# A fused attention and expert kernel: C times v over 128 tokens at a time, blocks of TensorE's instructions spaced by the plan, and landmark sums as trees of additions on VectorE

## The chip, the cores and the metric

The kernel runs on one core of one Trainium2 chip. The metric is the device time of the core in microseconds (us), so less is better. Most fast runs of one kernel agree within a per cent; a run that is over 1.5% above the fastest of the same kernel counts as slow. A *ratio* in this document is the mean time of one kernel's fast runs over the mean time of the other's fast runs of the same rounds on the same chip, so it isn't quite the ratio of the medians that stand beside it.

## The reference

A landmark attention (8 batches, 8 heads, 576 tokens, 64 features, 32 landmarks) feeds a mixture of 8 experts with one expert per token. Cut to what matters here:

```python
q_lm = q.reshape(B, H, 32, 18, D).mean(axis=3)      # landmark sums: 18 tokens each
k_lm = k.reshape(B, H, 32, 18, D).mean(axis=3)
A  = softmax(q @ k_lm.T);  Bm = softmax(q_lm @ k_lm.T);  C = softmax(q_lm @ k.T)
Z  = Bm.T / (norm1(Bm) * norminf(Bm))
for _ in range(6):
    Z = 2 * Z - Z @ Bm @ Z                           # the "W" chain, 6 steps
x = A @ Z @ C @ v                                    # C @ v: 32 x 576 times 576 x 64 per head
# then for each token: relu(x @ w1[e]) @ w2[e], scaled by a gate; e = argmax(x @ w_gate)
```

With the inputs used here all tokens of a batch go to one expert, and batches 2, 3 and 5 have the same expert as the batch two before, so their weight loads are skipped at run time (20 of 32 weight transfers are executed).

## The kernel before

The kernel isn't a loop written by hand. It lists its operations for all 8 batches with engine, estimated duration, what they read and write, and buffers; a small list scheduler in Python (the *plan*) then picks the order in which they are emitted, engine by engine. The instructions are unrolled, so TensorE executes one straight stream of about 9,400 records. A change of any number in the plan can reorder everything.

The scheduler's core takes, of the operations that can start first, the one with the best priority:

```python
for o in lst:
    s = max(f, o.ready)
    ...
    cands.append((s, o, picks))
...
order.sort(key=lambda o: o.start)
```

Landmark sums: one of two engines makes them, whichever the plan finds free. VectorE reduces the 18 tokens of each landmark with one strided instruction; GpSimd makes a tree of five additions through a scratch tile:

```python
def total(e, t=t, sums=sums, x=x):
    src = t.ap[:, 2 * x:2 * x + 2]
    if e == "DVE":
        nc.vector.tensor_reduce(sums.ap, src.rearrange("p j (x t) -> p j t x", x=g), axis=AX, op=ALU.add)
        return
    add = nc.gpsimd.tensor_tensor
    add(tr, src[:, :, 0:288], src[:, :, 288:576], op=ALU.add)
    for n in (128, 64, 32):
        add(tr[:, :, 0:n], tr[:, :, 0:n], tr[:, :, n:2 * n], op=ALU.add)
    add(sums.ap, tr[:, :, 0:32], tr[:, :, 256:288], op=ALU.add)
op(("DVE", "POOL"), {"DVE": 1.35, "POOL": 3.4}, "sum", total, ...)
```

C times v: nine chunks of 64 tokens. Two heads lie in the two halves of the partitions, so each matmul has 64 rows by 32 columns of the array:

```python
def flip(dst, c):                                    # transposes of C, 64 tokens of two heads at once
    nc.tensor.transpose(dst, in_=Cexp.ap[:, c].rearrange("p i t -> p (i t)"), identity=ident)
def valC(x):
    for c in (range(5) if x == 0 else range(5, 9)):
        src = Ct.ap if c == 4 else CT.ap[:, c // 5, 128 * (c % 5):128 * (c % 5) + 128]
        for j in range(J):                           # J = 4
            for i in range(I):                       # I = 2
                nc.tensor.matmul(pV.ap[quad(j), i, 0:D], lhsT=src[half(i), quad(j)], rhs=vt.ap[half(i), c, j, :],
                                 start=(c == 0), stop=(c == 8))
```

In the trace each of these fp32 matmuls stands as two weight loads and two matmuls: 72 matmuls a batch are 144 matmul records and 144 weight loads (1,152 of each in 8 batches), 288 instructions.

The softmax here doesn't subtract the row's maximum and nothing guards it: scores larger than these inputs give would overflow.

Of the kernel before, what the change touches and what calls it, by code (L numbers as in the profile page):

```python
# [22 lines left out]
F32 = mybir.dt.float32  # L23
# [5 lines left out]
ALU = mybir.AluOpType  # L29
# [25 lines left out]
class Op:  # L55
    __slots__ = ("eng", "dur", "lat", "fn", "deps", "succ", "new", "use", "kind", "b", "kb", "prio", "seq", "left", "start",
                 "end", "done", "ready", "tiled", "bias", "choice", "durs")


class Plan:  # L60


    LAT = {"PE": 0.27, "DVE": 0.09, "ACT": 0.12, "POOL": 0.12, "SP": 0.05}

    def __init__(self, model):
        self.ops, self.writer, self.m = [], {}, model

    def op(self, eng, dur, fn, kind, b, r=(), w=(), new=(), use=(), kb=0.0, tiled=False, bias=0.0):
        o = Op()
        deps = []  # L70
        for key in r:
            for p in self.writer[key]:
                if p not in deps:
                    deps.append(p)
        o.choice = eng if isinstance(eng, tuple) else (eng,)
        o.eng = o.choice[0]
        o.durs = {}
        for e in o.choice:
            o.durs[e] = self.m["dur"].get(kind + "@" + e, self.m["dur"].get(kind, dur[e] if isinstance(dur, dict) else dur))
        o.dur, o.lat, o.fn, o.deps, o.succ = o.durs[o.eng], self.LAT[o.eng], fn, deps, []  # L80
        o.new, o.use, o.kind, o.b, o.kb, o.seq, o.tiled, o.bias = list(new), list(use), kind, b, kb, len(self.ops), tiled, bias
        for t in o.new + o.use:
            t.users.append(o)
        for p in deps:
            p.succ.append(o)
        for key in w:
            self.writer.setdefault(key, []).append(o)
        self.ops.append(o)
        return o

    def run(self):
# [40 lines left out]
        n_left = len(ops)  # L132
        order = []
        slack = m["slack"]

# [30 lines left out]
        while n_left:  # L166
            best = None
            for e, lst in avail.items():
# [5 lines left out]
                for o in lst:  # L174
                    s = max(f, o.ready)
                    picks = ()
                    if first is not None and s > first + slack:
                        continue
                    if o.new:
                        rm = room(o)  # L180
                        if rm is None:
                            continue
                        s = max(s, rm[0])
                        picks = rm[1]
                    if o.kb and e == "SP" and len(lanes) >= m["lanes"]:
                        s = max(s, lanes[-m["lanes"]])
                    cands.append((s, o, picks))
                    if first is None or s < first:
                        first = s
# [16 lines left out]
            if o.eng == "PE" and o.tiled != pe_tiled:  # L206
                at += 0.09
                pe_tiled = o.tiled
            o.start, o.end = at, at + o.dur
            free[o.eng] = o.end  # L210
# [29 lines left out]

    def emit(self):
        for o in self.order:
            for t in o.new:
                t.make()
            o.fn() if len(o.choice) == 1 else o.fn(o.eng)


MODEL = {"period": 12.0, "stretch": 1.3, "slack": 0.1, "rate": 405.0, "lanes": 8,
         "dur": {"Mhi": 0.22, "expA": 0.66, "expB": 0.29, "expC": 0.52, "ezx": 0.28, 
                 "An": 0.76, "BT": 0.26, "P0": 0.23, "rd": 0.62, "upd": 0.29, "Mlo": 0.23,  # L250
                 "Cv0": 0.9, "Cv1": 0.72, "MT": 0.2, "Mg": 0.12, "Mw": 0.52, "W": 0.2, "colsum": 0.12, "gram": 0.16, "pG": 0.65,
                 "pb": 0.98, "pd": 0.58, "scC0": 0.68, "scC1": 0.55, "scA": 0.57},
         "off": {"H": 10, "Y": 10, "Y4": 10, "y": 10, "y4": 10, "st": 10}, "again": (2,)}
SPY = []
# [4 lines left out]
def attention_then_experts(ctx: ExitStack, tc, qt, kt, vv, gates, w, out):  # L259
# [29 lines left out]
    tag(sb, "qT", 3, [128, J, S])  # L289
    tag(sb, "v", 3, [128, 9, J, D])  # L290
    tag(sb, "ks", 6, [128, 2, m])
    tag(sb, "qs", 6, [128, 2, m])
    tag(sb, "Cexp", 1, [128, 9, I, 64])
    tag(sb, "CT", 1, [128, 2, 512])
# [57 lines left out]
    for e in range(E):  # L352
        nc.gpsimd.memset(iota8[:, e:e + 1], float(e))
    tr = cp.tile([128, 2, 288], F32)
    wg = cp.tile([128, J, 2 * E], F32)
# [37 lines left out]
    def batch(b):  # L393
# [8 lines left out]
        for x in range(2):  # L402
            for which, t, src in (("k", kT, kt), ("q", qT, qt)):
                def ld(t=t, src=src, x=x):
# [3 lines left out]
                    use=[t] if x else [])  # L408
        dma("ldv", lambda: nc.sync.dma_start(out=vt.ap.rearrange("p c j d -> p (c j d)"), in_=vv[b]), 128 * 2304 * 4, w=[("v", b)], new=[vt])
        if b == 0:  # L410
# [7 lines left out]
        for x in range(2):  # L418
            for which, t, sums in (("k", kT, ks[x]), ("q", qT, qs[x])):
                def total(e, t=t, sums=sums, x=x):  # L420
                    src = t.ap[:, 2 * x:2 * x + 2]
                    if e == "DVE":
                        nc.vector.tensor_reduce(sums.ap, src.rearrange("p j (x t) -> p j t x", x=g), axis=AX, op=ALU.add)  # L423
                        return
                    add = nc.gpsimd.tensor_tensor
                    add(tr, src[:, :, 0:288], src[:, :, 288:576], op=ALU.add)
                    for n in (128, 64, 32):
                        add(tr[:, :, 0:n], tr[:, :, 0:n], tr[:, :, n:2 * n], op=ALU.add)  # L428
                    add(sums.ap, tr[:, :, 0:32], tr[:, :, 256:288], op=ALU.add)
                op(("DVE", "POOL"), {"DVE": 1.35, "POOL": 3.4}, "sum", total, r=[(which, b, x)], w=[("s" + which, b)], new=[sums],  # L430
                   use=[t])
# [3 lines left out]

        CW = (320, 256)

        def score(lo, n, p, lm, tok, with_b):
# [4 lines left out]
            if with_b:  # L443
                for j in range(J):
                    for i in range(I):
                        nc.tensor.matmul(p.ap[quad(j), i, 320:320 + m], lhsT=qs[j // 2].ap[half(i), j % 2, :],
                                         rhs=ks[j // 2].ap[half(i), j % 2, :])
        for hf in range(2):
            op("PE", 0.65 if hf == 0 else 0.53, f"scC{hf}", lambda hf=hf: score(320 * hf, CW[hf], psC[hf], qs, kT, hf == 0),
               r=[("k", b), ("sq", b)] + ([("sk", b)] if hf == 0 else []), w=[("pC", b, hf)], new=[psC[hf]],  # L450
# [5 lines left out]
        for i in range(I):  # L456
            def expB(i=i):
                nc.scalar.activation(out=Bme.ap[:, i], in_=psC[0].ap[:, i, 320:320 + m], func=ACTF.Exp, scale=scale / (g * g),
                                     accum_out=st.ap[:, 4 + i:5 + i])
            op("ACT", 0.31, "expB", expB, r=[("pC", b, 0)], w=[("Bme", b)], new=[] if i else [Bme, st],  # L460
               use=[psC[0]] + ([Bme, st] if i else []))
        for hf in range(2):
            for i in range(I):
                def expC(hf=hf, i=i):
                    nc.scalar.activation(out=Cexp.ap[:, 5 * hf:5 * hf + CW[hf] // 64, i, :], in_=psC[hf].ap[:, i, 0:CW[hf]].rearrange(
                                             "p (c t) -> p c t", t=64), func=ACTF.Exp,
                                         scale=scale / g, accum_out=st.ap[:, 2 * hf + i:2 * hf + i + 1])
                op("ACT", 0.50, "expC", expC, r=[("pC", b, hf)] + ([("Bme", b)] if hf + i == 0 else []), w=[("Cexp", b, hf)],
# [71 lines left out]

        def flip(dst, c):
            nc.tensor.transpose(dst, in_=Cexp.ap[:, c].rearrange("p i t -> p (i t)"), identity=ident)  # L542
        for x in range(2):
            def turn(x=x):
                for c in range(4):
                    flip(pT.ap[:, x, 128 * c:128 * c + 128], 5 * x + c)
            op("PE", 0.48, "turn", turn, r=[("Cexp", b, x)], w=[("pT", b, x)], new=[] if x else [pT],
               use=[Cexp] + ([pT] if x else []))

            def cpy(e, x=x):  # L550
# [5 lines left out]
               new=[] if x else [CT], use=[pT] + ([CT] if x else []))  # L556
        op("PE", 0.15, "turn4", lambda: flip(at_[:, 0:128], 4), r=[("Cexp", b, 0)], w=[("pt", b)], new=[pt], use=[Cexp])
        op(EITHER, {"ACT": 0.27, "DVE": 0.29}, "Ct", lambda e: (nc.scalar.copy if e == "ACT" else nc.vector.tensor_copy)(
# [4 lines left out]
        def valC(x):  # L563
            for c in (range(5) if x == 0 else range(5, 9)):
                src = Ct.ap if c == 4 else CT.ap[:, c // 5, 128 * (c % 5):128 * (c % 5) + 128]
                for j in range(J):
                    for i in range(I):
                        nc.tensor.matmul(pV.ap[quad(j), i, 0:D], lhsT=src[half(i), quad(j)], rhs=vt.ap[half(i), c, j, :],  # L568
                                         start=(c == 0), stop=(c == 8))
        for x in range(2):  # L570
            op("PE", 1.1 - 0.2 * x, f"Cv{x}", lambda x=x: valC(x),
               r=[("CT", b, x), ("v", b)] + ([("pV", b, 0)] if x else [("Ct", b)]),
               w=[("pV", b, x)], new=[] if x else [pV], use=[CT, vt] + ([pV] if x else [Ct]), tiled=True)
        op("DVE", 0.3, "Cvn", lambda: nc.vector.tensor_tensor(
# [205 lines left out]
    plan.run()  # L780
    plan.emit()
    region.__exit__(None, None, None)
# [77 lines left out]
```

## Time and profile before

| | before |
|---|---|
| median, range of 4 runs | 289.74 us, 289.31 to 291.3 |
| profiled span, mean granted TensorE clock | 291.3 us, 0.895 |
| TensorE matmul busy | 231.7 us (80%) |
| TensorE records in order | 9,429 |
| stops at edges of 256 instructions (below) | 25.2 us |

The page of the profile, kernel before: the busy times with their share and instruction counts, the granted clock in 40 slices of the span (tenths), the chain of waits by engine, and three groups of instructions (busy time and mean ns of one, then the idle time of the engine before them and what ended it).

```profile
span 291.3 us, 10745 instructions
PE 231.7 (80%) x4685; PEld 135.7 (47%) x4686; DVE 168.1 (58%) x420; ACT 78.0 (27%) x240; POOL 62.7 (22%) x147
...
PEclk9999558857978999999589997999999979989997
...
PE 70%; DVE 11%; issue 11%; DMA 4%; ACT 2%; ACTq 0%
...
L568 PE MATMUL big<-v,CT 64*32 64x64 f32 x1024 | 15.4, 225 | 17.7 <-issue 17.7
...
L441 PE MATMUL big<-kT,qs 64*32 64x256 f32 (+1 forms) x256 | 16.1, 511 | 11.8 <-DVE qs L423 11.8
...
L423 DVE TENSOR_REDUCE qs<-qT 128x64 f32<-128x1152 f32 x11 | 23.4, 2123 | 0.0
```

TensorE is the busiest engine and the chain runs mostly through it. But 11% of the chain is "issue": time in which TensorE waited for nothing that the profile shows. Line 568, C times v, has most of it. Line 441, the scores, waits for the landmark sums, both times at the very start: the first eight matmuls begin at 9.1 us, the rest of the first scores at 13.1.

The waits of TensorE, kernel before (engine and line, what it waited for, us in total, times, longest):

```profile
PE big L568 <- issue: 18.6, 8, 4.5
PE big L441 <- DVE qs L423: 11.8, 2, 9.1
PE big L597 <- issue: 5.0, 2, 2.8
...
PE bank L520 <- issue: 1.6, 1, 1.6
```

One such wait in order of time, kernel before (start us, us, engine, line, tile, count, and in brackets the idle time):

```profile
25.20 0.81 PE L568 MATMUL big<-v,CT 64*32 64x64 f32 x59
30.00 0.43 PE L568 MATMUL big<-v,CT 64*32 64x64 f32 x5 [3.99 <-issue]
```

TensorE stops for 4 us in the middle of a group of like matmuls, which makes a missing operand unlikely. If all TensorE records are sorted by start and numbered from 0, all eleven issue gaps over 0.3 us come before record numbers that leave 193 when divided by 256 (worked out from the trace's records):

```
record   705  1729  2497  2753  3777  5057  6081  6337  7361  8385  8641
mod 256  193   193   193   193   193   193   193   193   193   193   193
gap us  3.99  1.59  0.36  4.46  0.86  3.28  2.06  2.76  0.97  2.62  2.25     sum 25.2
```

That is the reading: TensorE stops at the edge of a block of 256 instructions. The trace has a DMA queue of the kind "instruction" that fits it: 39 packets of 16,384 bytes, 0.9 to 2 us each, for 37 edges. Most start 0.1 to 4 us after an edge, a few only shortly before the next. And at each of the eleven stops TensorE resumes 1.3 to 1.5 us after the end of such a packet (for the first: the packet ends at 28.67 us, TensorE resumes at 30.00), while edges without a stop lie anywhere from 0.5 to 10.6 us behind the newest packet (the last edge, near the end, 20.7). How long TensorE took for a block, the stop left out, can be worked out from the same records: all six blocks that took under 3 us ended in a stop, and none that took over 5.7 us did. So, in this reading, a block executed too quickly ends before the next one is there.

### The profile page before, as it was taken

The numbers are of one execution on the slowest core, as the hardware profiler recorded it, in microseconds if no ns is written. First come the engines' busy times: TensorE is split into PE (matmuls) and PEld (weight loads), VectorE is DVE, ScalarE is ACT, GpSimd is POOL, SyncE is SP. The second block draws the span as 40 slices with busy tenths as digits, with TensorE's granted clock in tenths as the row PEclk, the third lists the DMA queues.
The fourth block names the chain that finished last, engine by engine and source line by source line (L and its number), as shares of the span: only waits on it lengthen the run. The fifth ranks groups of instructions, "written<-read, shape, count | busy, mean of one in ns | idle before, by whom it ended". The sixth has DMA issues, their size and how long they took to land.

```text
span 291.3 us, 10745 instructions
## 1 busy us (share of the span) xinstructions
PE 231.7 (80%) x4685; PEld 135.7 (47%) x4686; DVE 168.1 (58%) x420; ACT 78.0 (27%) x240; POOL 62.7 (22%) x147
## 2 busy tenths in 40 slices
PE   0385586689769998995999949998999399599890
PEld 0134444444444556544655636456645364253440
DVE  3774566785429678575286615664766154354730
ACT  1041032044201362231242504231605041220400
POOL 7386209257440008004001200000020002100000
PEclk9999558857978999999589997999999979989997
DMA  7999929957990484347402980130039602963132
GB/s 264 418 415 412 415 59 303 296 160 213 267 281 19 149 301 141 145 135 284 164 2 88 198 169 7 37 129 4 2 84 229 144 3 38 246 174 115 47 110 65
DMA packets 14601, 49.06 MB, mean 168 GB/s; under 512 B 1744, under 2 KB 2768, under 8 KB 13520
## 3 DMA queue, kind: packets, MB, share of 16 engines
q1 hardware_dynamic: 11664, 37.79, 34.7%
q0 software_dynamic: 2880, 10.49, 18.9%
q8 instruction: 39, 0.64, 0.9%
q14 instruction: 18, 0.15, 0.2%
HBM read 61.90 MB, written 9.44 MB: 245 GB/s over the span
## 4 chain that ended last, share of the span: by engine, by line
PE 70%; DVE 11%; issue 11%; DMA 4%; ACT 2%; ACTq 0%
PE mo L376 18%; PE mo L722 14%; PE big L441 7%; PE bank L520 6%; PE big L568 5%; PE big L597 4%; DVE ks L423 4%; PE mo L386 3%; PE big L542 3%; DVE qs L423 3%; PE mo L379 3%; DMA out_dram<-y 2%; PE bank L648 2%; PE bank L586 2%; DMA kT<-in_kt_dram 1%
## 5 line engine op out<-in xcount | busy, mean ns | idle before, releaser
L376 PE MATMUL mo<-wb,hT 128*128 128x512 bf16 x256 | 60.6, 383 | 0.1
L722 PE MATMUL mo<-A,P 128*128 128x288 f16 x256 | 48.7, 336 | 1.3 <-ACT P L713 0.7
L728 ACT ACTIVATE hT<-mo 128x288 bf16<-128x288 f32 x67 | 27.4, 411 | 64.4 <-PE mo L722 63.0
L376 PEld LDWEIGHTS <-hT 128*128 128x128 bf16 x256 | 23.5, 99 | 26.9 <-issue 2.3
L730 DVE TENSOR_SCALAR hT<-mo 128x288 bf16<-128x288 f32 x61 | 27.8, 457 | 14.1 <-PE mo L722 12.9
L748 DVE TENSOR_SCALAR y<-mo,cmain 128x512 f32<-128x512 f32 (+1 forms) x34 | 24.4, 717 | 18.8 <-PE mo L376 16.5
L722 PEld LDWEIGHTS <-P 128*128 128x128 bf16 x256 | 26.2, 112 | 17.5 <-issue 6.1
L568 PE MATMUL big<-v,CT 64*32 64x64 f32 x1024 | 15.4, 225 | 17.7 <-issue 17.7
L698 POOL COPY cmain<-coef 128x5 f32 x8 | 1.5, 190 | 118.9 <-DVE coef L696 94.8
L520 PE MATMUL bank<-cur 32*32 32x64 f32 (+1 forms) x768 | 21.4, 229 | 5.4 <-issue 1.6
L441 PE MATMUL big<-kT,qs 64*32 64x256 f32 (+1 forms) x256 | 16.1, 511 | 11.8 <-DVE qs L423 11.8
L524 DVE SCALAR_TENSOR_TENSOR cur<-cur,bank 128x128 f32<-128x128 f32 (+1 forms) x48 | 13.0, 271 | 20.5 <-PE bank L520 16.3
L423 DVE TENSOR_REDUCE qs<-qT 128x64 f32<-128x1152 f32 x11 | 23.4, 2123 | 0.0
L520 PEld LDWEIGHTS bank<-cur 32*32 32x32 f32 x768 | 13.4, 112 | 20.7 <-issue 4.6
L568 PEld LDWEIGHTS big<-v,CT 64*32 64x32 f32 x1024 | 11.6, 105 | 20.6 <-issue 18.9
L428 POOL TENSOR_TENSOR tr<-tr 128x256 f32<-128x256 f32 (+2 forms) x39 | 19.5, 500 | 3.1
L602 DVE TENSOR_TENSOR A<-Aexp,big 128x576 f16<-128x576 f32 x16 | 11.8, 748 | 14.0 <-PE big L597 14.0
L713 ACT CAST P<-mo 128x512 bf16<-128x512 f32 x16 | 9.4, 585 | 37.1 <-PE mo L386 37.0
L423 DVE TENSOR_REDUCE ks<-kT 128x64 f32<-128x1152 f32 x8 | 17.1, 2132 | 3.7 <-DMA kT<-in_kt_dram 3.7
L597 PE MATMUL big<-rd,bsel 32*128 32x72 f32 x256 | 13.9, 363 | 5.1 <-issue 5.0
L597 PEld LDWEIGHTS big<-rd,bsel 32*128 32x128 f32 x256 | 12.1, 262 | 7.4 <-issue 5.4
L386 PE MATMUL mo<-wb,Mt 64*32 64x512 bf16 x256 | 11.8, 410 | 3.5 <-ACT y L746 2.6
(98 smaller groups left out, 274.6 us busy)
## 6 DMA issues: line engine op xcount, KB each, us to landing
wb<-in_w_dram POOLq DMA_DIRECT2D x32, 512.0 KB
kT<-in_kt_dram SPq DMA_DIRECT2D x16, 576.0 KB, 5.7
qT<-in_qt_dram SPq DMA_DIRECT2D x16, 576.0 KB, 10.1
v<-in_vv_dram SPq DMA_DIRECT2D x8, 1152.0 KB, 8.9
out_dram<-y SPq DMA_DIRECT2D x32, 256.0 KB, 2.1
out_dram<-y SPq DMA_DIRECT2D x8, 128.0 KB, 3.9
wg<-in_gates_dram SPq DMA_DIRECT2D x1, 32.0 KB, 11.8
```

Of the source, the lines that this page charges most:

```text
L376: nc.tensor.matmul(pY, lhsT=lhsT, rhs=w2[:, fc, :], start=(fc == 0), stop=(fc == FC - 1))
L386: nc.tensor.matmul(pP[i][quad(j), :], lhsT=Mt[half(i), b, x, j, :], rhs=w1[half(i), fh, j, :], start=(x == 0), stop=(x == 1))
L423: nc.vector.tensor_reduce(sums.ap, src.rearrange("p j (x t) -> p j t x", x=g), axis=AX, op=ALU.add)
L428: add(tr[:, :, 0:n], tr[:, :, 0:n], tr[:, :, n:2 * n], op=ALU.add)
L441: nc.tensor.matmul(p.ap[quad(j), i, 0:n], lhsT=lm[j // 2].ap[half(i), j % 2, :], rhs=tok.ap[half(i), j, lo:lo + n])
L520: nc.tensor.matmul(spv(0, 2 * m)[quad(r), i, lo:], lhsT=src.ap[quad(r), i, 0:m], rhs=src.ap[quad(r), i, lo:])
L568: nc.tensor.matmul(pV.ap[quad(j), i, 0:D], lhsT=src[half(i), quad(j)], rhs=vt.ap[half(i), c, j, :], start=(c == 0), stop=(c == 8))
L597: nc.tensor.matmul(pb[i].ap[:, hf, QS * s:QS * s + QS], lhsT=bsel[qd, s].rearrange("p a b -> p (a b)"), rhs=rd.ap[qd, :])
L722: nc.tensor.matmul(pH.ap[:, 0:HS], lhsT=P.ap[:, i, fc * 128:fc * 128 + 128], rhs=A[:, b, i, HS * hf:HS * hf + HS], start=(i == 0), stop=(i ...
L728: nc.scalar.activation(out=o, in_=pH.ap[:, 0:HS], func=ACTF.Relu)
L730: nc.vector.tensor_scalar(out=o, in0=pH.ap[:, 0:HS], scalar1=0.0, scalar2=None, op0=ALU.max)
L748: nc.vector.tensor_scalar(out=y.ap[:, 0:wd], in0=pY.ap[:, 0:wd], scalar1=cmain[:, b, c:c + 1], scalar2=None, op0=ALU.mult)
```

## The change

It has three parts.

1. C times v over 128 tokens at a time. Four chunks of 128 tokens and a rest of 64 replace nine of 64, with the layouts of v, C and the transposes changed to suit (also on the host). A batch has 160 instructions for it instead of 288.
2. The plan: it counts TensorE's instructions, and delays in its model any operation that would cross an edge of 256 less than 3.6 us after the edge before, so that others go first. It makes later batches' sums less urgent (`pen`), and knows that the weight loads of batches 2, 3 and 5 are skipped, not that of 2 alone.
3. VectorE makes its landmark sums by the tree of five unit-stride additions too, with its own scratch tile.

The diff, cut to its core:

```diff
+    INS = {"scC0": 64, "scC1": 32, "scA": 32, ..., "Cv0": 64, "Cv1": 96, ...}   # instructions of an operation
+        o.ins, o.pen = self.INS.get(kind, 0) + 1, pen * self.m["pen"]
+        block, fetch = 256, m["fetch"]
+        count, crossed = 0, 0.0
+        def stall(o, at):
+            if o.eng != "PE" or count // block == (count + o.ins) // block:
+                return 0.0
+            return max(0.0, crossed + fetch - at - o.dur * (block - count % block) / o.ins)
+                    if e == "PE":
+                        s += stall(o, s)
+                    s += o.pen
-MODEL = {..., "again": (2,)}
+MODEL = {..., "fetch": 3.6, "fill": (0.0, 0.7, 0.08), "pen": 0.5, ..., "again": (2, 3, 5)}   # this fill emits nothing
...
-                    if e == "DVE":
-                        nc.vector.tensor_reduce(sums.ap, src.rearrange("p j (x t) -> p j t x", x=g), axis=AX, op=ALU.add)
-                        return
-                    add = nc.gpsimd.tensor_tensor
+                    add, tr = (nc.vector if e == "DVE" else nc.gpsimd).tensor_tensor, trs[e]
-                op(("DVE", "POOL"), {"DVE": 1.35, "POOL": 3.4}, "sum", total, ...
+                op(("DVE", "POOL"), {"DVE": 1.5, "POOL": 3.6}, "sum", total, pen=1.0 if b else 0.0, ...
...
-        CW = (320, 256)
+        CW = (256, 320)
-    nc.tensor.transpose(dst, in_=Cexp.ap[:, c].rearrange("p i t -> p (i t)"), identity=ident)
+    nc.tensor.transpose(dst, in_=Cexp.ap[:, i, lo:lo + n], identity=ident)
+        def turn4():                                  # the last 64 tokens, one matmul per head
+            for i in range(I):
+                nc.tensor.matmul(at_[half(i), 0:128], lhsT=Cexp.ap[:, i, 512:576], rhs=ident)
...
-            for c in (range(5) if x == 0 else range(5, 9)):
+            for c in (range(2) if x == 0 else range(2, 5)):
                 for j in range(J):
                     for i in range(I):
+                        if c == 4:
+                            nc.tensor.matmul(o, lhsT=Ct.ap[half(i), quad(j)], rhs=vt.ap[half(i), 2048 + D * j:...], ...)
+                        else:
+                            lo = 256 * (c % 2) + 128 * i + m * j
+                            nc.tensor.matmul(o, lhsT=CT.ap[:, x, lo:lo + m], rhs=vt.ap[:, 512 * c + 256 * i + D * j:...], ...)
```

## The prediction

> **What bounds it now.** By the busy table TensorE takes 231.7 of 291.3 us (80%), VectorE 58%. The chain of waits is 70% TensorE, 11% VectorE and 11% "issue" (about 31 us). The waits view names the issue time: 18.6 us before the C times v matmuls, 5.0 before the spread of the row sums, 1.6 before a W step. Numbering TensorE's records in order, eleven gaps (0.4 to 4.5 us, 25.2 us in all) stand at numbers that leave 193 when divided by 256: TensorE stops at the edge of a block of 256 instructions. [...] 39 packets of 16,384 bytes on an instruction queue, each about 1 us. [...] A stopped edge follows the edge before by mostly 4.8 to 6.7 us. C times v, 288 instructions a batch in about 2.2 us, empties a block faster than one is fetched.
>
> **What changes.**
> 1. C times v: 144 to 80 matmuls a batch. Before, 15.1 ns each (64 in 0.97 us). The new form (128 rows by 32 columns, 64 moving) resembles the row sums (32 in 0.64 us, 20 ns at 72): estimate 18 ns, so 2.2 to about 1.4 us; the last transpose grows by about 0.2 us. -4.5 us in all.
> 2. Instructions: about -120 of 1,180 a batch, four fewer edges in all and a shorter burst: transposes, row sums, C times v and spread go from 434 to 320.  Stops: 25 to about 7 us, so -18.
> 3. The plan's block counter starts at zero and counts one extra per operation, about 50 a batch, where the trace has about 7 semaphore records a batch and the first edge at record 193. So its edges drift from the true ones; I credit the spacing with little.
> 4. Landmark sums on VectorE: 19 reductions of 2.13 us. A five-step tree, estimated from the 0.15 to 0.75 us of other additions, is about 1.6 us. But both inputs lie in SBUF: [...] the Bme addition took 0.77 us instead of 0.22 beside GpSimd's trees, a 2-element addition 0.71 instead of 0.15. GpSimd's selects run until 9 us, its trees until 138: I expect the gain to vanish: 0, give or take 2 us. The first scores still begin near 13 us.
> 5. Fewer stops may keep the clock up (mean grant 0.895; about 50 us at half after the start): -2 us.
>
> These are on the chain, so nearly all counts: 289.9 - 18 - 4.5 - 2 + 1.5 (new waits on VectorE and ScalarE) = 267 us.
>
> **Prediction: 267 us, 256 to 281. Faster by over 2%: 0.93; within 2%: 0.06; slower: 0.01.**
>
> **To check.** C times v records 640 instead of 1,152, about 11 us of chain; issue idle on TensorE below 10 us, what is left at edges of 256; VectorE's first tree additions (128x576) near 0.7 us alone, over 1 us beside GpSimd; the last 40 us (two experts' dense matmuls) unchanged.
>
> **What would make it wrong.** The edges fall badly and stops of 3 to 4 us stay; blocked trees delay the W chain; or the new order starves the experts' matmuls of weights, or the clock is halved more often.

289.9 - 18 - 4.5 - 2 + 1.5 comes to 266.9. The 2 us of item 5 are an estimate beside two figures of the trace. What before's trace shows of it: up to the last matmul there are seven half-clock stretches, 58 us in all. Six begin during one of the eleven stops or at most 0.5 us after it, the seventh 1.7 us after a wait of 2.6 us for ScalarE; beside the other five stops (0.4 to 2.6 us) the clock records stand at 1.0.

## The result

| | before | after |
|---|---|---|
| median, range of 4 runs | 289.74 us, 289.31 to 291.3 | 275.5 us, 274.2 to 276.49 |
| ratio | | 0.950 (95%: 0.944 to 0.955) |
| profiled span, clock | 291.3 us, 0.895 | 274.3 us, 0.924 |
| TensorE records | 9,429 | 8,452 |
| stops at edges | 25.2 us | 7.7 us |

The kernel is 5% faster, inside the predicted range, 8.5 us above the predicted median. The page after (line numbers have moved: 599 is C times v, 464 the scores; 449 the tree's first addition, 451 its next three):

```profile
span 274.3 us, 9860 instructions
PE 220.1 (80%) x4197; PEld 127.2 (46%) x4198; DVE 160.9 (59%) x462; ACT 80.0 (29%) x244; POOL 86.4 (31%) x177
...
PEclk9999579759997999999979997999999759999999
...
PE 68%; DVE 17%; issue 5%; POOL 4%; ACT 3%; POOLq 0%; DVEq 0%; ACTq 0%
...
L464 PE MATMUL big<-kT,qs 64*32 64x256 f32 (+1 forms) x256 | 15.5, 528 | 14.5 <-POOL qs L452 14.5
...
L451 DVE TENSOR_TENSOR trDVE<-trDVE 128x256 f32<-128x256 f32 (+2 forms) x39 | 20.1, 515 | 1.3
```

Issue on the chain fell from 11% to 5%, but VectorE on it rose from 11% to 17%, and GpSimd came onto it with 4%. C times v no longer stands with idle time, as its group by form shows (kernel after):

```profile
L599 PE MATMUL big<-v,CT 128*32 128x64 f32 x512 | 11.0, 223 | 0.7 <-ACT CT L577 0.4 <-issue 0.3
```

The waits of TensorE, kernel after:

```profile
PE big L464 <- POOL qs L452: 14.5, 1, 14.5
PE bank L542 <- issue: 6.7, 4, 3.7
PE big L644 <- DVE A L634: 4.3, 4, 3.0
PE mo L402 <- DVE y L780: 3.6, 1, 3.6
PE big L662 <- DVE Mt L652: 2.7, 2, 2.0
```

The first scores now wait for a sum by GpSimd until 14.5 us (before: for VectorE's, until 9.1 us for the first eight matmuls and 13.1 for the rest), and there are new waits of 3 to 4 us on VectorE. The plan also moved sums: VectorE makes 13 of the 32 and GpSimd 19, where it was 19 and 13 before. The longest, for an output scaling (y), ends at 86 us. VectorE in order of time just before it, kernel after:

```profile
77.17 0.75 DVE L449 TENSOR_TENSOR trDVE<-qT 128x576 f32<-128x576 f32 x1
77.95 2.57 DVE L451 TENSOR_TENSOR trDVE<-trDVE 128x256 f32<-128x256 f32 x3
80.62 0.43 DVE L452 TENSOR_TENSOR qs<-trDVE 128x64 f32<-128x64 f32 x1
81.08 0.90 DVE L449 TENSOR_TENSOR trDVE<-kT 128x576 f32<-128x576 f32 x1
82.02 2.56 DVE L451 TENSOR_TENSOR trDVE<-trDVE 128x256 f32<-128x256 f32 x3
84.61 0.50 DVE L452 TENSOR_TENSOR ks<-trDVE 128x64 f32<-128x64 f32 x1
85.04 0.34 DVE L652 TENSOR_TENSOR Mt<-big,Mt 128x64 bf16<-128x64 f32 x2
85.30 2.05 DVE L780 TENSOR_SCALAR y<-mo,cmain 128x512 f32<-128x512 f32 x3
```

and GpSimd in the same time, kernel after:

```profile
77.32 0.78 POOL L452 TENSOR_TENSOR ks<-trPOOL 128x64 f32<-128x64 f32 x1
78.17 1.46 POOL L449 TENSOR_TENSOR trPOOL<-kT 128x576 f32<-128x576 f32 x1
79.72 1.65 POOL L451 TENSOR_TENSOR trPOOL<-trPOOL 128x256 f32<-128x256 f32 x3
81.45 0.71 POOL L452 TENSOR_TENSOR ks<-trPOOL 128x64 f32<-128x64 f32 x1
82.24 1.46 POOL L449 TENSOR_TENSOR trPOOL<-qT 128x576 f32<-128x576 f32 x1
```

Two sums took VectorE from 77.17 to 85.11 us, 7.9 us, where two reductions take 4.2 (experiment 1). The two engines take turns: GpSimd's 64-element addition takes 0.78 us instead of 0.32, as it ends only after VectorE's first (at 77.92 us); VectorE's middle three take 2.57 us, as they sit behind GpSimd's 1.46 us. All 13 trees of VectorE in this trace, put in order by how long GpSimd executed an instruction that reads SBUF (where the operands of both engines' additions lie) beside them (worked out from the records):

```
beside GpSimd us   0.00  0.00  0.00  0.00 | 1.76  1.95  1.99 | 2.51  2.72 | 3.43  3.49  3.55  3.64
the tree took us   2.05  2.05  2.05  2.12 | 2.34  2.17  2.21 | 2.90  3.11 | 3.89  3.88  3.94  4.03
```

A tree by itself takes 2.05 us, and the reduction it replaces 2.13. So it gains next to nothing alone, and costs up to 1.9 us beside GpSimd. (The 1.95 and 1.99 are short GpSimd selects at the start; there it was GpSimd that was held up, its 16 selects of line 375 took 6.7 us instead of 5.6.) Not every instruction of VectorE was held up: before's 19 reductions took 2.08 to 2.20 us with up to 2.1 us of GpSimd beside them, and the 16 instructions A<-Aexp,big of the kernel after, which take one input from a tile that TensorE writes, 0.74 to 0.76 us with and without GpSimd.

The idle time of TensorE in both traces, all worked out from the matmul records (first start, gaps between, end):

| us | before | after | change | the prediction's term |
|---|---|---|---|---|
| stops at edges | 25.2 | 7.7 | -17.5 | -18 |
| matmuls busy | 231.7 | 220.1 | -11.6 | -4.5 and -2 (clock) |
| other idle up to the last matmul | 27.4 | 40.9 | +13.5 | +1.5 |
| after the last matmul | 7.1 | 5.5 | -1.5 | |
| span | 291.3 | 274.3 | -17.0 | -23 |

Each number is rounded by itself. The table compares one profiled run of each kernel, and before's, at 292.9 us, was 3.2 us above its median: the medians differ by 14.2 us, not by 17. A stop is any gap over 0.3 us at an edge; one of after's, 1.05 us, is put down to ScalarE by the profile.

### The profile page after: what moved, and what is told of

Its sections match the earlier page's. It is cut to its first block, busy times and chain, and to the rows that moved or that the text cites. A ratio compares the mean times of both kernels' runs of the same rounds, so it can differ in the third digit from the quotient of the medians.

```text
span 274.3 us, 9860 instructions
## 1 busy us (share of the span) xinstructions
PE 220.1 (80%) x4197; PEld 127.2 (46%) x4198; DVE 160.9 (59%) x462; ACT 80.0 (29%) x244; POOL 86.4 (31%) x177
## 4 chain that ended last, share of the span: by engine, by line
PE 68%; DVE 17%; issue 5%; POOL 4%; ACT 3%; POOLq 0%; DVEq 0%; ACTq 0%
PE mo L402 20%; PE mo L754 11%; PE big L464 8%; PE bank L542 6%; DVE trDVE L451 5%; PE big L629 3%; PE mo L405 3%; PE mo L412 3%; PE big L564 3%; PE big L599 3%; DVE hT L762 2%; DVE trDVE L449 2%; POOL bsel L375 2%; PE bank L680 2%; PE bank L618 2%
## 5 line engine op out<-in xcount | busy, mean ns | idle before, releaser
L754 PE MATMUL mo<-A,P 128*128 128x288 f16 x256 | 44.7, 306 | 4.6 <-DVE hT L762 2.2
L754 PEld LDWEIGHTS <-P 128*128 128x128 bf16 x256 | 23.2, 103 | 18.8 <-issue 10.0
L451 POOL TENSOR_TENSOR trPOOL<-trPOOL 128x256 f32<-128x256 f32 (+2 forms) x57 | 29.9, 525 | 4.5
L702 POOL DMA_DIRECT2D wb<-in_w_dram x24 | 6.9, 289 | 72.1 <-DMA wb<-in_w_dram 56.6
L464 PE MATMUL big<-kT,qs 64*32 64x256 f32 (+1 forms) x256 | 15.5, 528 | 14.5 <-POOL qs L452 14.5
L546 DVE SCALAR_TENSOR_TENSOR cur<-cur,bank 128x128 f32<-128x128 f32 (+1 forms) x48 | 12.9, 269 | 18.9 <-PE bank L542 9.1
L451 DVE TENSOR_TENSOR trDVE<-trDVE 128x256 f32<-128x256 f32 (+2 forms) x39 | 20.1, 515 | 1.3
L449 POOL TENSOR_TENSOR trPOOL<-qT 128x576 f32<-128x576 f32 x13 | 18.8, 1449 | 0.7 <-issue 0.2
L481 ACT ACTIVATE Bme<-big 128x32 f32<-128x32 f32 x16 | 3.0, 193 | 44.1 <-PE big L469 44.1
L488 ACT ACTIVATE Cexp<-big 128x256 f32<-128x256 f32 (+1 forms) x32 | 12.9, 412 | 4.2 <-PE big L464 4.2
L778 ACT ACTIVATE y<-mo,cmain 128x256 f32<-128x256 f32 (+1 forms) x10 | 5.6, 560 | 27.8 <-PE mo L405 20.1
L743 DVE CAST P<-mo 128x512 bf16<-128x512 f32 x16 | 10.9, 684 | 4.4 <-PE mo L412 4.3
```

What stands on the lines that cost most here:

```text
L464: nc.tensor.matmul(p.ap[quad(j), i, 0:n], lhsT=lm[j // 2].ap[half(i), j % 2, :], rhs=tok.ap[half(i), j, lo:lo + n])
L488: nc.scalar.activation(out=Cexp.ap[:, i, 256 * hf:256 * hf + CW[hf]], in_=psC[hf].ap[:, i, 0:CW[hf]], func=ACTF.Exp, scale=scale / g, accu ...
L546: nc.vector.scalar_tensor_tensor(out=dst.ap[:, :, lo:], in0=src.ap[:, :, lo:], scalar=2.0, in1=spv(0, 2 * m)[:, :, lo:], op0=ALU.mult, op1 ...
L754: nc.tensor.matmul(pH.ap[:, 0:HS], lhsT=P.ap[:, i, fc * 128:fc * 128 + 128], rhs=A[:, b, i, HS * hf:HS * hf + HS], start=(i == 0), stop=(i ...
```

## Experiments

Theory 1: the stops are instruction fetch at edges, the short C times v removed them, and the trees on VectorE gave back about 10 us because they and GpSimd's trees exclude each other. Rivals: the stops are waits for C times v's operands; the gain is the plan's spacing; the new waits come of the new order. Three calls of four kernels, each on one chip, with the kernel before run beside them. Medians below are of fast runs. In the first call (experiments 1 to 4) 3 of 8 runs of before were slow, in the third (9 to 12) 4 of 7; there the record's verdict is "unclear" for the kernels that have a ratio, and runs 2 and 12, each with two slow runs of four, have none. In the second call (5 to 8) all four kernels are "faster".

### 1. After, with reductions on VectorE, order unchanged

```diff
+                    if e == "DVE":
+                        nc.vector.tensor_reduce(sums.ap, src.rearrange("p j (x t) -> p j t x", x=g), axis=AX, op=ALU.add)
+                        return
                     add, tr = (nc.vector if e == "DVE" else nc.gpsimd).tensor_tensor, trs[e]
```

> The kernel after, with its order of instructions unchanged, but each landmark sum that VectorE makes is the single strided reduction of before again (13 of them). Theory 1 (the trees' two SBUF inputs exclude GpSimd's trees, so VectorE is blocked and the new waits of TensorE on VectorE are paid for by that): the reductions take 2.1 us each whatever GpSimd does, GpSimd's first additions go back to 1.41 us, the first scores start near 13 us instead of 14.5, and the whole takes 268 to 273 us against 275.5. Rival (the new waits come of the new order, the trees themselves gain 0.3 to 0.6 us each): 276 to 280 us.

Measured: 265.4 us (264.5 to 268.2), ratio to before 0.917 (0.908 to 0.926), against 0.950 (0.944 to 0.955) for the kernel after in another call: the intervals don't touch. GpSimd's first additions take 1.41 us again (1.87 for the first of them in the kernel after), and the first scores begin at 12.9 us, though they wait for the same sum by GpSimd as in the kernel after:

```profile
PE big L467 <- POOL qs L455: 12.9, 1, 12.9
```

The place of the two sums on VectorE, this kernel:

```profile
74.45 2.13 DVE L449 TENSOR_REDUCE qs<-qT 128x64 f32<-128x1152 f32 x1
76.51 2.14 DVE L449 TENSOR_REDUCE ks<-kT 128x64 f32<-128x1152 f32 x1
78.58 0.34 DVE L655 TENSOR_TENSOR Mt<-big,Mt 128x64 bf16<-128x64 f32 x2
78.84 2.05 DVE L783 TENSOR_SCALAR y<-mo,cmain 128x512 f32<-128x512 f32 x3
```

Two sums take 4.2 us instead of 7.9. As the order is the same, the two streams of weight loads can be laid on each other: the trees' kernel is 1.6 us behind at the first score, 2.7 us at 76 us, 7.3 us at 88 us, 11.2 at 141 us, after GpSimd's last trees, and 11.7 at the end. So theory 1 holds, and more strongly than expected: the time is below my 268 to 273. Of the 11.4 us between the two spans, 8.1 are idle time of TensorE, and 4.9 are matmul busy time (34 us at half clock against 41); stops are 1.4 longer. Two half-clock stretches that only the trees' kernel has, 86.0 to 89.4 us and 137.2 to 140.6, begin at or just after the end of a stop in which TensorE waits for VectorE behind a tree (3.6 us until 86.09, 2.2 until 136.07). Whether the stops caused them isn't shown.

### 2. Before, with trees on VectorE, order unchanged

```diff
-                    if e == "DVE":
-                        nc.vector.tensor_reduce(...)
-                        return
-                    add = nc.gpsimd.tensor_tensor
+                    add, tr = (nc.vector if e == "DVE" else nc.gpsimd).tensor_tensor, trs[e]
```

> The kernel before, order unchanged, but each sum on VectorE is the tree of five additions (19 of them). Theory 1 (blocking): the first tree additions on VectorE take over 0.9 us where a GpSimd tree runs; the first scores start no earlier than 12 us; 289 to 294 us in all. Rival (the tree is a gain of about 0.5 us for each of the sums, most of which are on the chain): 282 to 286 us.

Measured: 291.5 us (fast: 290.7 and 292.4; two slow runs at 296), before 291.1. No gain for 19 trees, as theory 1 said, and the rival's 282 to 286 is out. First scores begin at 9.4 and 13.7 us, 0.3 and 0.6 later than before; I had said no earlier than 12. Thirteen of the 19 trees had at most 2.1 us of GpSimd beside them and took 2.05 to 2.32 us; the worst, beside 3.67 us of GpSimd, took 4.05. Against reductions of 2.13 us the 19 trees took VectorE 8.3 us more in all, nearly the 9.0 us of the 13 trees in the kernel after. In this trace TensorE's other idle time is 33.4 us, 6 more than before's, but matmuls are busy 3.6 us less and stops 1.9 us shorter. So the trees weren't free here either; the rest made up for them, and one trace of each can't say whether by chance. That the same part costs nothing in the total of one order and 10 us in another is worth remembering.

### 3. Before, with the edges moved by half a block

```diff
+        for _ in range(64):
+            filler()          # nc.tensor.matmul(bank[0:32, 384:385], lhsT=onesb[:, 0:32], rhs=onesb[:, 0:1])
         for o in self.order:
```

> The kernel before with 64 tiny matmuls (128 records) ahead of everything, in the time when TensorE waits for the first data. They move the edges of the blocks of 256 by half a block against the program. Theory (stops stand at the edges of instruction blocks): all issue gaps over 0.3 us still stand at record numbers that leave 193 when divided by 256, which is now at other instructions; their sum changes, 15 to 32 us; the time 283 to 297 us. Rival (they are waits for an operand of C times v): the gaps stay at the same matmuls of the program, now 65 over a multiple of 256, and the time stays within 1 us of 289.7.

Measured: 288.6 us, ratio 0.991 (0.980 to 1.002). All twelve issue gaps stand at numbers that leave 193 or 194 (this trace lacks a few matmul records, so it is numbered by its weight loads), 24.9 us in all, but now they come before other instructions. The waits of TensorE, this kernel:

```profile
PE big L570 <- issue: 12.0, 4, 4.1
PE big L443 <- DVE qs L425: 9.1, 2, 6.4
PE bank L522 <- issue: 6.1, 3, 3.3
PE bank L588 <- issue: 5.6, 3, 2.8
```

Line 588 is the row sums, which hadn't one issue gap before, and 522 the W chain. The program's instructions and operands are the same; only their numbers differ. So the stops belong to the numbers and not to C times v: what C times v does is to make the blocks short in time. The operand rival falls. The time decides nothing here; the places of the gaps do.

### 4. After, without the spacing

```diff
-"fetch": 3.6
+"fetch": 0.0
```

> The kernel after with the plan's spacing of blocks turned off (its fetch time set to 0), all else as it is. Theory (the plan's edges drift from the true ones, the win is from fewer instructions): stops at edges sum to 5 to 14 us and the time is 272 to 281 us. Rival (the spacing is what removed the stops): stops of 18 us or more and 284 to 290 us.

Measured: 280.6 us, ratio 0.966 (0.959 to 0.972); stops 7.8 us, with spacing 7.7. The spacing isn't what removed the stops. The kernel is still 5 us slower than the one after (in another call), at the same stops. Its order is another one: in the traces 3.1 us of the difference are matmul busy time (51 us at half clock against 41) and 2.3 us other idle time. So the spacing was worth something here, but not by its stops.

### 5. Before, with C times v over 128 tokens alone

The layouts, transposes, widths and matmuls of the change; sums, costs and plan settings as before.

In words:

```diff
 (of the kernel after)
-"fetch": 3.6 ... "pen": 0.5 ... "again": (2, 3, 5)
+"fetch": 0.0 ... "pen": 0.0 ... "again": (2,)
 and the reduction of experiment 1, with {"DVE": 1.35, "POOL": 3.4}
```

> The kernel before with one part of the change alone: C times v over 128 tokens (its layouts, transposes and score widths), with the landmark sums, the costs and the plan settings of before. Theory (shorter instruction bursts are the gain, the trees a loss): stops at edges fall from 25 to 10 us or less, C times v records from 1,152 to 640, 264 to 275 us, so at least as good as the whole change. Rival (the parts need each other, the plan's spacing above all): stops over 15 us, 278 us or more.

Measured: 264.9 us, ratio 0.905 (0.901 to 0.910); the profiled run was a slow one (268.3). Stops 8.8 us. The waits of TensorE, this kernel:

```profile
PE big L467 <- DVE qs L449: 12.0, 2, 9.1
PE bank L545 <- DVE rd L624: 4.1, 6, 2.3
PE big L632 <- issue: 3.8, 3, 2.3
PE big L598 <- issue: 3.3, 1, 3.3
```

Blocks that took TensorE under 3 us: two, both with a stop, where before had six. From before's trace to this one stops fall by 16.4 us and matmul busy time by 10.7, other idle time grows by 3.7. One part alone gives more than the whole change.

### 6. Before, with the plan part alone

```diff
+spacing (3.6 us; "turn4": 2, "Cv0": 160, "Cv1": 128), "pen": 0.5, "again": (2, 3, 5)
```

> The kernel before with the plan part alone: spacing of blocks at 3.6 us with counts for the old C times v, delay of later batches' sums, and the three skipped weight loads known. Theory (its edges drift from the true ones and 288 instructions of C times v can't be spaced): stops at edges 18 us or more, 283 to 292 us. Rival (spacing works by itself): stops under 12 us, 280 us or less.

Measured: 277.3 us, ratio 0.947 (0.941 to 0.953); stops 15.3 us (a slow run's trace). A miss: I expected 283 to 292 and stops of 18 or more. The time is the rival's (280 or less), the stops (under 12) are nobody's. On the old kernel the plan part does work.

### 7 and 8. The plan told the truth, without and with edges where the trace has them

Both are the kernel of experiment 1 with the first batch's sums held on VectorE and a reduction costed at 2.05 us; the second has besides:

```diff
-o.ins = self.INS.get(kind, 0) + 1;    count, crossed = 0, 0.0;   "fetch": 3.6
+o.ins = self.INS.get(kind, 0) + 0.13; count, crossed = 67, 0.0;  "fetch": 5.4
```

> The kernel after with VectorE's sums as single reductions, the plan told what such a one takes (2.05 us), and the first batch's four sums held on VectorE, because in the kernel after one of them went to GpSimd, which is busy with constants until 9 us. Theory: the first scores begin by 13.3 us; about even with the same kernel without this (265.4 us), 261 to 268 us; stops at edges 4 to 14 us, as the order is new. Rival (the order of after is what made 265 possible): over 270 us.

> As the run before, and the plan's edges put where the trace has them: the counter starts at 67 instead of 0, counts 0.13 instead of 1 extra per operation, and an edge costs 5.4 us instead of 3.6. Theory (the spacing did little because its edges were in the wrong places): stops at edges under 4 us in all and 2 to 8 us less than the run before. Rival (the order can't be spaced: too little else is ready in the bursts): stops within 3 us of the run before, and no gain.

Measured: 266.4 us (ratio 0.909, 0.906 to 0.913) without, 268.8 us (0.917, 0.912 to 0.921) with. Stops 9.1 us in both. With the sums held on VectorE the first eight matmuls of the scores begin at 8.9 us and the rest at 12.9, where experiment 1 has all at 12.9; the whole gained nothing by it. The expectation of stops under 4 us is a miss, and the rival holds: with edges in the right places the plan still can't space them. One stop shows why. In every kernel with the new C times v the longest stop is one of 3.2 to 3.7 us at the last batch's C times v; the kernel after:

```profile
212.97 0.68 PE L599 MATMUL big<-v,CT 128*32 128x64 f32 x32
213.59 0.34 PE L595 MATMUL big<-v,Ct 64*32 64x64 f32 x16
217.67 0.43 PE L542 MATMUL bank<-cur 32*32 32x32 f32 x16 [3.73 <-issue]
```

It stays with and without spacing, and with either count of edges (3.4 and 3.6 us). That too little other work was ready there is my reading; no run shows it.

### 9 and 10. Spacing alone, and the known skips alone, on the kernel before

```diff
+"fetch": 3.6                                  (run 9, "pen": 0.0, "again": (2,))
-"again": (2,)
+"again": (2, 3, 5)                            (run 10)
```

> The kernel before with the plan's spacing of blocks alone (3.6 us, counts for the old C times v), neither the delay of the sums nor the three known skips. The whole plan part gave 14.7 us, against my theory. Theory 2 (spacing works although its edges drift, because it breaks up the bursts anywhere): most of that gain is here, stops at edges 12 to 18 us, 276 to 283 us. Rival (the gain is of the other two settings): stops over 22 us, 286 us or more.

> The kernel before with one setting changed: the plan knows that the weight loads of batches 2, 3 and 5 are skipped, not of 2 alone. Theory 2 (the gain of the plan part is the spacing): within 3 us of before, stops at edges 20 to 30 us. Rival (knowing the skips lets the experts' matmuls come earlier and fill the bursts): 279 to 285 us, stops under 20 us.

Measured: spacing alone 283.2 us, ratio 0.978 (0.961 to 0.996), stops 19.4 us, where I said 276 to 283 and 12 to 18: both just missed. Known skips alone 280.8 us, ratio 0.979 (0.958 to 1.000), before 290.6; stops 22.3 us. That's a miss: I had said within 3 us of before. The rival's time (279 to 285) fits, its stops (under 20) don't. Both settings help the old kernel about equally, and the first reduces stops by about 6 us. The second's gain is mainly in matmul busy time, 221.3 us against 231.7, with the clock at half for 34 us instead of 58 us (clock records of the trace, from the first matmul to the last; the stretch before the first record, at 21 to 22 us, isn't counted). Why the order keeps the clock up was not tried.

### 11 and 12. With the new C times v: without and with the plan part, on one chip

Both have reductions on VectorE, costed at 2.05 us; the second has spacing, `pen` and the three skips.

```diff
-{"DVE": 1.35, "POOL": 3.4}      (run 11: of experiment 5)     -{"DVE": 1.5, "POOL": 3.6}   (run 12: of experiment 1)
+{"DVE": 2.05, "POOL": 3.4}                                    +{"DVE": 2.05, "POOL": 3.4}
```

> C times v over 128 tokens alone (the plan settings of before, reductions on VectorE), the plan told that a reduction takes 2.05 us instead of 1.35. Theory (C times v is the whole gain): 262 to 270 us. It is the partner of the next run on the same chip.

> As the run before plus the whole plan part (spacing, delay of sums, three known skips). Theory (with the short C times v the plan part adds nothing clear: the bursts are already short, stops stay at 7 to 11 us in both): within 3 us of the run before. Rival (the parts add up, the plan part was worth 14.7 us on the kernel before): 5 us or more below it, stops under 4 us.

Measured: 265.8 us without (four runs from 265.2 to 266.3; ratio to before 0.919, 0.907 to 0.931). With the plan part the two fast runs are 267.0 and 270.1, and two slow ones 271.8 and 273.2: no gain, perhaps a small loss. Stops 9.3 and 6.5 us. The parts don't add up: what the plan part was worth on the old kernel isn't there to be had once C times v is short.

### All together

| kernel | fast median us | ratio to before | stops us |
|---|---|---|---|
| after (all three parts) | 275.5 | 0.950 | 7.7 |
| trees alone (2) | 291.5 | fast medians as before's | 23.3 |
| plan alone (6) | 277.3 | 0.947 | 15.3 |
| C times v alone (5) | 264.9 | 0.905 | 8.8 |
| C times v and plan (1) | 265.4 | 0.917 | 9.1 |
| C times v, reduction costed right (11) | 265.8 | 0.919 | 9.3 |

Ratios of different calls use different runs of before (fast medians 289.7, 291.1, 293.1 and 290.6 us), so differences of a per cent between calls decide nothing. All three of the last beat both kernels given, and the simplest of them is C times v alone.

## Why the prediction was right, and where it was off

The prediction was 267 us (256 to 281), the result 275.5. Direction, range and main mechanism held.

- *What bounds it.* Right. Experiment 3 shows that the gaps stand at edges of 256 instructions whatever instruction is there.
- *Stops 25 to about 7 us.* Right: 7.7. The mechanism, fewer and less bunched instructions, is shown by experiment 5 (C times v alone, 8.8; blocks of under 3 us fell from six to two).
- *C times v -4.5 us.* Mis-sized: its matmuls were busy 17.2 us before and 13.2 after, the transposes of the last 64 tokens grew from 2.7 to 3.5: -3.2 in all. A new matmul took 20 ns (31 in 0.62 us) where I had estimated 18. These figures, like the 15.1 ns of before, spread the whole of a group's last matmul (0.22 us) over the group; from start to start 80 old ones followed each other every 10 ns (0.82 us), 32 new ones every 15 (0.47 us).
- *The clock -2 us.* Mis-sized. Matmul busy time fell by 11.6 us, of which 3.2 is the item above; the other 8.4 come with 41 us at half clock instead of 58 (I had put before's at about 50). The clock records of both traces are all 1.0 or 0.5, in whole multiples of 3.413 us but for the last, which is cut. Whether fewer stops caused it isn't shown; experiment 10 had 34 us at half clock with stops of 22.3 us.
- *Trees: "the gain to vanish: 0, give or take 2 us. The first scores still begin near 13 us."* This is the step that failed. The collision itself was read rightly from before's trace (additions of 0.77 us instead of 0.22 and 0.71 instead of 0.15), and in the trace of after the two engines take turns (GpSimd's addition of 0.78 us instead of 0.32, VectorE's middle three of 2.57). But I priced a tree at 1.6 us, where it takes 2.05 alone and up to 4.03 blocked, and I added nothing for the new order, in which trees of both engines lie side by side. The first scores began at 14.5 us, 1.6 us later than in experiment 1, where they wait for the same sum of GpSimd behind the same constants: the difference is the collision, in which GpSimd's selects of line 375 took 6.7 us instead of 5.6 and its first addition 1.87 instead of 1.41. Replacing the trees by reductions in the same order took 11.4 us off the span. The term "new waits +1.5" measured +13.5, of which 8.1 go away with the trees (other idle time up to the last matmul is 32.8 us in experiment 1, against 40.9) and the rest, 5.4, is the new order's with reductions. What it consists of was not taken apart.
- *Little credit for the spacing.* Right for the stops of this change (7.8 without, 7.7 with); but without it the kernel took 280.6 us, so the order that came with it was worth some 5 us, and on the old kernel it gives about 2%.
- *Known skips, which I left out.* Alone on the old kernel they gave about 2% or a little more; with the new C times v the plan part as a whole added nothing clear.

The total was helped by luck: idle time 12 us over its term was partly made good by busy time 5 us and an end 1.5 us under theirs, by amounts that I hadn't foreseen. The sum 267 is nearer to the kernel with reductions (265.4) than to the one predicted.

What stays open: why the new order without spacing is 5 us slower at equal stops (experiment 4), what sets the half-clock windows, and how far the instruction packets can run ahead of TensorE: two edges of before were crossed without a stop 0.5 and 0.6 us after the end of a packet, where every stop ended 1.3 to 1.5 us after one.

## What to carry to other kernels

If an engine stands still for nothing the profile names, number its instructions: here the gaps stood at one remainder of 256, and ended 1.3 to 1.5 us after a packet of the instruction queue. The remedy was fewer instructions in the burst, which took 16 us of stops away; the part that did it gave 9% alone. A change that bundles parts can be worth less than one of them: undo each part in the unchanged order before keeping all. Before an operation is moved to another form on VectorE, look at what GpSimd executes at that time: here the two engines took turns, and a tree took up to 4.03 us instead of 2.05, where reductions stayed at 2.08 to 2.20.
